# Image scale modulation of a joint image-text attention block: from thin matmul columns to column-tiled rows that VectorE turns into columns

## The chip, the cores and the metric

The kernel runs on one core of a Trainium2 chip. TensorE (PE) does the matmuls and the PE transposes, VectorE (DVE) and ScalarE (ACT) do the elementwise work and empty PSUM, GpSimd (POOL) does small fills, and SyncE (SP) issues nearly all DMAs. The metric is the device time of one execution in microseconds (us), the median of several runs; lower is better. Dates such as "at 14.39" are microseconds from the start of the profiled span.

## What is computed

The sizes are B = 2 batches, 256 image tokens, 32 text tokens, D = 1152 = 9 × 128, all in bfloat16. For the image side (the text side is the same with its own weights):

```
mod  = silu(c) @ wmod_img                 # six vectors of D per batch; three are used
sh, sc, ga = mod[0], mod[1], mod[2]       # shift, scale, gate
h    = layernorm(x_img) * (1 + sc) + sh
q, k, v = split(h @ wqkv_img)
```

Text and image q, k and v are joined, softmax(q k^T / sqrt(D)) v is formed, and each side ends with `out = x + ga * (a @ wo)`. Every weight matrix is read once from HBM; 40.86 MB move in one execution.

## The kernel before, in words

**Weights.** A weight tile is `[128 partitions, 9, 1152]`: "row kt" of a tile below means the 128 rows of the matrix with index kt (288 KB), all 1152 columns. Five slots (`w0` to `w4`) are used in turn. SP issues the loads in program order (lines 103 to 122): two for `x_img`, four for the scale weights `w_sc_i` (rows 0-3, 4-6, 7 and 8), four for the image V weights `w_v_i` (row 0, rows 1-2, rows 3-5, rows 6-8), then one whole tile each for the image shift weights `w_sh_i`, for `w_q_i`, and so on. A load into a slot that was used before waits until its readers are done.

**Modulation columns.** `c` comes in as 18 rows, goes through silu on ACT, and one PE transpose makes it columns: `sT` holds `[128, 9, 2]`, one column per (kt, batch). `sT32` is the same padded to 32 columns with zeros. `sc_cols` (line 214) makes 1 + sc in the form "feature on the partition": for each row kt of `w_sc_i` nine matmuls of a 128×128 block of weights with the two moving columns of `sT`. A first matmul, of a matrix of 1/128 with ones, puts the 1 into PSUM. The result `sc_ps` is `[128, 9, 2]` in PSUM.

The shift goes another way: `mod_rows_of` (line 309) uses `sT32[:, kt, :]` as stationary matrix (32 columns) and lets the weights stream as moving operand. The array is split into four column strips of 32; strip g takes the columns that lie in quarter g of each 128, 288 in all, and writes partitions 32g to 32g+31. A DVE transpose of 32×32 blocks (`mod_cols_of`, line 317) then turns these rows into columns `[128, 9, 32]`, of which the first two are the batches.

**Image tokens.** Four token tiles of 128 are normalised (`xn_i`), batch 0 first. `x_transposes(k0, b)` (line 223) turns three feature blocks of one batch by six PE transposes into a PSUM tile, and returns the function that copies this tile to `xT_i` (ACT, or DVE for k0 = 3). These PSUM tiles alternate between two buffers (`ps_tr`), so the third tile of batch 1 takes the buffer of its first, and its transposes wait for that copy. `x_scale(k0, k1, b)` (line 237) multiplies `xT_i` by 1 + sc on DVE, one instruction per feature block, and writes `hS_i`. The shift is not added there: V is computed without it, and `sh @ w_v` is added later.

**V.** `v_open` (line 247) multiplies `hS_i` by `w_v_i`, 512 output columns a matmul, into PSUM accumulators. `A0` names the four of batch 0, `A1` two of batch 1. The order, lines 281 to 301, is written out by hand:

```
    sc_cols(4, 7)
    out01 = x_transposes(0, 1)
    sc_cols(7, K8); sc_cols(K8, KT)        # K8 = 8, KT = 9
    out31 = x_transposes(3, 1)
    out01(); x_scale(0, 3, 0, sc_ps); sc1_i <- sc_ps
    v_open(A0, 0, 3)
    out61 = x_transposes(6, 1)
    out31(); out61(); the other x_scale
    v_open(A1, 0, 3); v_open(A0 + A1, 3, 7); ...
```

`pin` (line 58) keeps an instruction in program order among the pinned ones; all matmuls and transposes on PE and most of the early DVE and ACT work are pinned, while `mod_cols_of` is not. `warm_up(n)` (line 136) is n matmuls of a constant tile whose result nobody reads; they stand where PE would idle.

**Afterwards** the shift is made from `w_sh_i` and added (`xT_i` becomes the modulated input), V is finished, then come q and k (`qk_img`), the text side, whose shift is formed on DVE while PE works on q and k, then scores, softmax, attention output and output projection. In the text side `txt_cols_shift` and `txt_modulate` (lines 431 to 445) call `mod_cols_of` too and build `hT_t`, which the text q and k matmuls read.

Of the kernel before, what the change touches and what calls it, by code (L numbers as in the profile page):

```python
# [9 lines left out]
ALU = mybir.AluOpType  # L10
# [4 lines left out]
def kernel(  # L15
# [14 lines left out]
    nc = tc.nc  # L30
    bf = mybir.dt.bfloat16
    f32 = mybir.dt.float32
    PSUM = bass.MemoryType.PSUM

    B, NI, D = x_img.shape
    NT = x_txt.shape[1]
    P = 128
    KT = D // P
# [13 lines left out]
    const = ctx.enter_context(tc.tile_pool(name="const", bufs=1))  # L52
    work = ctx.enter_context(tc.tile_pool(name="work", bufs=2))
    small = ctx.enter_context(tc.tile_pool(name="small", bufs=4))
    ps_mm = ctx.enter_context(tc.tile_pool(name="ps_mm", bufs=6, space=PSUM))
    ps_tr = ctx.enter_context(tc.tile_pool(name="ps_tr", bufs=2, space=PSUM))

    pin = tc.keep_in_program_order

    def mm(*a, **k):  # L60
        return pin(nc.tensor.matmul(*a, **k))  # L61

    def tr(*a, **k):
        return pin(nc.tensor.transpose(*a, **k))  # L64
# [11 lines left out]
    def wtile(slot):  # L76
        return wpool.tile([P, KT, D], bf, tag="w%d" % slot, name="t")
# [4 lines left out]
    K8 = KT - 1  # L82
# [17 lines left out]
    w_sc_i = wtile(0)  # L100
# [5 lines left out]
    SCC = (0, 4, 7, K8, KT)  # L106
    for r0, r1 in zip(SCC, SCC[1:]):
        nc.sync.dma_start(w_sc_i[:, r0:r1, :], sc_v[:, r0:r1, :])  # L108
    for r0, r1 in ((0, 1), (1, 3), (3, 6), (6, KT)):
        nc.sync.dma_start(w_v_i[:, r0:r1, :], v_v[:, r0:r1, :])  # L110
    w_sh_i = load_w(2, wmod_img, 0)
    w_q_i = load_w(3, wqkv_img, 0)
# [12 lines left out]
    eps_t = eps_row[:, 0:1]  # L125
    nc.vector.memset(eps_row[:], EPS)
    warm = const.tile([P, 512], bf)
    nc.vector.memset(warm[:], 0.0)  # L128
    unit = const.tile([P, P + B * KT], bf)
    nc.gpsimd.memset(unit[:, 0:P], 1.0 / P)  # L130
    nc.gpsimd.memset(unit[:, P:], 1.0)
    ident = const.tile([P, P], bf)
    make_identity(nc, ident[:])
    wps = ps_mm.tile([P, 512], f32, tag="mm")
# [1 line left out]
    def warm_up(n):  # L136
        for _ in range(n):
            mm(wps[:], lhsT=warm[:, 0:P], rhs=warm[:], start=True, stop=True)

    warm_up(8)  # L140
    sT32 = const.tile([P, KT, 32], bf)
# [15 lines left out]
    sT_ps = ps_tr.tile([P, B * KT], bf, tag="tr")  # L157
    tr(sT_ps[:], s18[:], ident[0:B * KT, 0:B * KT])
    sT = const.tile([P, KT, B], bf)
    warm_up(17)  # L160

    def silu_cols():
        pin(nc.vector.tensor_copy(sT[:], sT_ps[:].rearrange("p (b kt) -> p kt b", b=B)))
# [42 lines left out]
    hS_i = act.tile([P, KT, B * NI], bf, tag="Bt")  # L206
    xT_i = act.tile([P, KT, B * NI], bf)

    sc1_i = const.tile([P, KT, B], f32)
    qkT = act.tile([P, 2 * KT, B, NTOK], bf, tag="Q")  # L210

    sc_ps = ps_mm.tile([P, KT, B], f32, tag="mm")

    def sc_cols(r0, r1):
        if r0 == 0:
            mm(sc_ps[:].rearrange("p kt b -> p (kt b)"), lhsT=unit[:, 0:P], rhs=unit[:, P:],
               start=True, stop=False, skip_group_check=True)
        for kt in range(r0, r1):
            for j in range(KT):
                mm(sc_ps[:, j, :], lhsT=w_sc_i[:, kt, j * P:(j + 1) * P], rhs=sT[:, kt, :],  # L220
                   start=False, stop=(kt == KT - 1), skip_group_check=True)

    def x_transposes(k0, b):
        tr_pool = b == 1 or k0 < 6
        tp = (ps_tr if tr_pool else ps_mm).tile([P, 3, NI], bf, tag="tr" if tr_pool else "mm", name="tp")
        for kt in range(k0, k0 + 3):
            for t in range(TPB):
                i = b * TPB + t
                tr(tp[:, kt - k0, t * P:(t + 1) * P], xn_i[:, i, kt * P:(kt + 1) * P], ident[:])
        dst = xT_i[:, k0:k0 + 3, b * NI:(b + 1) * NI]  # L230

        def copy_out():
            pin(nc.vector.tensor_copy(dst, tp[:]) if k0 == 3 else nc.scalar.copy(dst, tp[:]))

        return copy_out

    def x_scale(k0, k1, b, sc=None):
        sc = sc1_i if sc is None else sc
        for kt in range(k0, k1):
            pin(nc.vector.tensor_scalar(hS_i[:, kt, b * NI:(b + 1) * NI], xT_i[:, kt, b * NI:(b + 1) * NI],  # L240
                                        sc[:, kt, b:b + 1], None, op0=ALU.mult))

    VW = 512
    v_i = act.tile([P, NIT, D], bf, tag="A")
# [2 lines left out]
    def v_open(ids, k0, k1, kt_major=True):  # L247
        for key in ids:
            if key not in accs:
                accs[key] = ps_mm.tile([P, VW], f32, tag="mm", name="vps")  # L250
        loop = [(kt, key) for kt in range(k0, k1) for key in ids] if kt_major else \
            [(kt, key) for key in ids for kt in range(k0, k1)]
        for kt, (i, cc) in loop:
            mm(accs[(i, cc)][:], lhsT=hS_i[:, kt, i * P:(i + 1) * P], rhs=w_v_i[:, kt, cc * VW:(cc + 1) * VW],
               start=(kt == 0), stop=(kt == KT - 1), skip_group_check=True)
            if kt == KT - 1:
                evac(v_i[:, i, cc * VW:(cc + 1) * VW], accs[(i, cc)][:])
# [20 lines left out]
    ln_norm(x_i[:, 2, :], s2[:, 0:1], r2, P, xn_i[:, 2, :])  # L278
    for out in [x_transposes(k0, 0) for k0 in (0, 3, 6)]:
        out()  # L280
    sc_cols(0, 4)
    warm_up(5)
    sc_cols(4, 7)
    out01 = x_transposes(0, 1)
    sc_cols(7, K8)
    sc_cols(K8, KT)
    out31 = x_transposes(3, 1)
    out01()
    x_scale(0, 3, 0, sc_ps)
    pin(nc.vector.tensor_copy(sc1_i[:], sc_ps[:]))  # L290
    v_open(A0, 0, 3)
    out61 = x_transposes(6, 1)
    out31()
    out61()
    for k0 in (0, 3, 6):
        for b in range(B):
            if k0 or b:
                x_scale(k0, k0 + 3, b)
# [1 line left out]
    v_open(A0 + A1, 3, KT - 2)  # L300
    v_open(A0 + A1, KT - 2, KT, kt_major=False)

    NGG = 4
    LW = P // NGG

    def group(w, kt, g):
        return w[:, kt, :].rearrange("p (c g l) -> p g c l", g=NGG, l=LW)[:, g]

    def mod_rows_of(w, lhs):
        gps = ps_tr.tile([P, KT, LW], f32, tag="tr")  # L310
        for kt in range(KT):
            for g in range(NGG):
                mm(gps[LW * g:LW * g + LW], lhsT=lhs[:, kt, :], rhs=group(w, kt, g),
                   start=(kt == 0), stop=(kt == KT - 1), tile_position=(0, LW * g))
        return gps

    def mod_cols_of(gps, name):
        t = const.tile([P, KT, LW], f32, name=name)
        nc.vector.transpose(t[:].rearrange("p c l -> p (c l)"), gps[:].rearrange("p c l -> p (c l)"))
        return t  # L320

    v_open([(2, 1)], 0, KT)
    p_sh = mod_rows_of(w_sh_i, sT32)
    sh_i = mod_cols_of(p_sh, "shc")
    nc.vector.tensor_copy(shT32[:, :, 0:B], sh_i[:, :, 0:B])
    hT_i = xT_i
    for kt in range(KT):
        for b in range(B):
            h = hT_i[:, kt, b * NI:(b + 1) * NI]
            if b == 0 or kt % 3 == 0:  # L330
                nc.vector.tensor_scalar(h, h, sc1_i[:, kt, b:b + 1], sh_i[:, kt, b:b + 1],
                                        op0=ALU.mult, op1=ALU.add)
# [19 lines left out]
    def qk_img(wq, blk, hooks):  # L352
        for j in range(KT):
# [3 lines left out]
            for kt in range(KT):  # L357
# [4 lines left out]
    gsc = tc.dram_tile([2, B, D], bf, name="mod_scratch")  # L362
    sel = const.tile([P, NGG, NTT], bf)
    nc.gpsimd.tensor_scalar(sel[:].rearrange("p g (b t) -> p g b t", b=B),
                            ident[:].rearrange("p (g r) -> p g r", g=NGG)[:, :, 0:B].unsqueeze(3)
                            .to_broadcast([P, NGG, B, NT]), -1.0, None, op0=ALU.mult)
    v_t = act.tile([P, D], bf)
    nc.gpsimd.memset(v_t[NTT:P, :], 0.0)
    svr = act.tile([P, KT, LW], bf)
    rows, cols = {}, {}  # L370

    def shift_v_rows():
        p_sv = mod_rows_of(w_v_i, shT32)
        nc.scalar.copy(svr[:], p_sv[:])
        cols["v"] = mod_cols_of(p_sv, "svc")
# [55 lines left out]
    def txt_cols_shift():  # L431
        cols["sh"] = mod_cols_of(rows["sh"], "shtc")
        nc.vector.tensor_copy(mod_t[:, 0], cols["sh"][:, :, 0:B])
# [26 lines left out]
    def v_txt():  # L460
        for r in range(2):
            ps = ps_mm.tile([P, KT, LW], f32, tag="mm")
            for kt in range(KT):
                for g in range(2):
                    mm(ps[64 * g:64 * g + NTT], lhsT=hT_t[:, kt, :], rhs=group(w_v_t, kt, 2 * r + g),
                       start=(kt == 0), stop=False, tile_position=(0, 64 * g))
            for g in range(2):
                mm(ps[64 * g:64 * g + NTT], lhsT=sel[:, 2 * r + g, :], rhs=svr[:],
                   start=False, stop=True, tile_position=(0, 64 * g))
            for g in range(2):  # L470
                evac(v_t[0:NTT, :].rearrange("p (c g l) -> p g c l", g=NGG, l=LW)[:, 2 * r + g],
                     ps[64 * g:64 * g + NTT])
# [201 lines left out]
```

## Time and profile before

| What | Value |
|---|---|
| Median of 6 runs | 121.54 us (121.17 to 122.17) |
| The profiled execution's own time | 121.27 us |
| Its span | 119.5 us |
| PE busy | 113.9 us (95%), 1105 matmuls |
| DVE, ACT, POOL busy | 74.0, 42.3, 11.6 us |
| Bytes moved, mean rate | 40.86 MB, 342 GB/s |
| PE first matmul of V | at 14.40 |
| PE last matmul chain | ends at 115.48 |

The profile is one execution. Its span of 119.5 us leaves 1.77 us of the execution's own 121.27 us outside, and this execution lies 0.27 us under the median. A busy PE in the table means that matmuls were under way. A single matmul of 512 columns shows 379 ns, but they overlap, and a stream of them starts one every 215 ns; so rates are read from stretches, not from the duration of one. "SPq" is the queue in which SP issues DMAs. A DMA's landing is the issue time plus its time to landing.

### The profile page before, as it was taken

How to read it: one execution, taken by the hardware profiler on the slowest of the kernel's cores; microseconds unless marked ns; L12 is line 12 of the kernel's file. 1: busy time of each engine (PE TensorE's matmuls, PEld its weight loads, DVE VectorE, ACT ScalarE, POOL GpSimd, SP SyncE). 2: the span in 40 equal slices, each digit the busy share in tenths (PEclk: the TensorE clock that was granted, in tenths of full speed). 3: DMA queues.
4: the chain of work that ended last, by engine and by line, in shares of the span. 5: the costliest groups of instructions: out<-in, count | busy, mean ns of one | idle time of the engine just before them, and what ended most of it. 6: DMA issues, size and time to landing. Idle time of an engine off the chain costs nothing.

```text
span 119.5 us, 2609 instructions
## 1 busy us (share of the span) xinstructions
PE 113.9 (95%) x1105; PEld 66.9 (56%) x1105; DVE 74.0 (62%) x155; ACT 42.3 (35%) x86; POOL 11.6 (10%) x34
## 2 busy tenths in 40 slices
PE   5999999999999999999999999999999999999980
PEld 2346744445574444445444457886777766567660
DVE  1568492053867799999999700017785746666670
ACT  4799402031662523323049132335347610000000
POOL 8240000000000000000000000000210806200000
PEclk9999999999999999999999999999999999999999
DMA  3999999999999999999999999999999992420222
GB/s 125 380 378 395 403 404 414 410 412 413 402 404 394 400 411 412 410 413 413 413 405 410 411 414 410 409 410 403 416 408 403 413 383 76 157 99 0 99 67 81
DMA packets 18517, 40.86 MB, mean 342 GB/s; under 512 B 923, under 2 KB 1451, under 8 KB 18507
## 3 DMA queue, kind: packets, MB, share of 16 engines
q1 hardware_dynamic: 17632, 39.56, 85.0%
q0 software_dynamic: 480, 0.89, 2.0%
q10 hardware_dynamic: 395, 0.26, 0.7%
q8 instruction: 8, 0.13, 0.4%
q14 instruction: 2, 0.02, 0.0%
HBM read 39.38 MB, written 1.34 MB: 341 GB/s over the span
## 4 chain that ended last, share of the span: by engine, by line
PE 84%; DMA 8%; SPq 2%; DVE 2%; issue 1%; DVEq 0%
PE ps L61 52%; PE vps L61 14%; DMA t<-in_wmod_img_dram 8%; PE aps L61 6%; PE gps L61 6%; PE sps L61 4%; SPq L108 1%; DVE hS_i L240 1%; PE pT_ps L64 1%; SPq L104 1%; DVE tmp L615 1%; DVE o L616 0%; PE sc_ps L61 0%; PE tpt L64 0%; PE tp L64 0%
## 5 line engine op out<-in xcount | busy, mean ns | idle before, releaser
L61 PE MATMUL ps<-xT_i,t 128*128 128x512 bf16 x162 | 35.8, 379 | 0.0
L61 PEld LDWEIGHTS <-t 128*128 128x128 bf16 x405 | 22.7, 98 | 20.1 <-DMA t<-in_wmod_img_dram 0.9
L398 DVE SCALAR_TENSOR_TENSOR acc_sh<-t,sTf,acc_sh 128x1152 f32<-128x1152 bf16 x16 | 21.3, 1401 | 0.0
L61 PE MATMUL ps<-t,aT 128*128 128x384 bf16 (+3 forms) x153 | 20.2, 308 | 0.0
L61 PE MATMUL vps<-t,hS_i 128*128 128x512 bf16 (+1 forms) x108 | 18.2, 326 | 0.4 <-DVE hS_i L240 0.3
L61 PEld LDWEIGHTS <-aT 128*128 128x128 bf16 (+1 forms) x153 | 13.0, 101 | 7.1 <-issue 0.5
L61 PEld LDWEIGHTS <-hS_i 128*128 128x128 bf16 x108 | 8.9, 98 | 9.0 <-issue 0.8
L615 DVE TENSOR_TENSOR tmp<-ps,gb 128x384 bf16<-128x384 f32 (+2 forms) x13 | 6.8, 526 | 6.3 <-PE ps L61 5.0
L348 ACT ACTIVATE qkT<-ps 128x512 bf16<-128x512 f32 (+2 forms) x11 | 6.2, 563 | 12.3 <-PE ps L61 12.3
L483 POOL DMA_DIRECT2D mod_scratch<-g_sb x4 | 2.5, 634 | 78.4 <-ACT g_sb L173 78.4
L61 PE MATMUL wps<-warm 128*128 128x512 bf16 x30 | 8.3, 433 | 1.2 <-DVE warm L128 1.2
L350 ACT CAST qkT<-ps 128x512 bf16<-128x512 f32 (+2 forms) x11 | 5.9, 554 | 8.6 <-PE ps L61 8.6
L171 DVE CAST v_i<-vps 128x512 bf16<-128x512 f32 x5 | 3.5, 691 | 7.6 <-PE vps L61 7.6
L171 DVE CAST v_t<-ps 64x288 bf16<-64x288 f32 x2 | 0.9, 459 | 11.7 <-ACT v_t L173 11.7
L61 PE MATMUL aps<-pT,v_i 128*128 128x288 bf16 x36 | 6.7, 287 | 0.0
L587 DVE TENSOR_SCALAR aT<-aps,svc 128x288 bf16<-128x288 f32 x9 | 4.7, 518 | 2.4 <-PE aps L61 2.3
L61 PEld LDWEIGHTS <-warm 128*128 128x128 bf16 x30 | 3.0, 109 | 5.0 <-issue 1.6
L61 PE MATMUL sps<-qkT 128*128 128x288 bf16 (+1 forms) x54 | 5.5, 287 | 0.0
L589 ACT ACTIVATE aT<-aps,svc 128x288 bf16<-128x288 f32 x9 | 4.5, 501 | 2.5 <-PE aps L61 2.5
L61 PE MATMUL aps<-pT,v_t 128*128 128x288 bf16 x18 | 5.1, 286 | 0.0
L61 PE MATMUL gps<-t,sT 128*32 128x288 bf16 x144 | 5.1, 287 | 0.0
L61 PE MATMUL ps<-hT_t,t 128*128 128x64 bf16 x162 | 5.0, 193 | 0.0
(106 smaller groups left out, 108.7 us busy)
## 6 DMA issues: line engine op xcount, KB each, us to landing
t<-in_wqkv_txt_dram SPq DMA_DIRECT2D x3, 2592.0 KB, 15.7
t<-in_wmod_img_dram SPq DMA_DIRECT2D x2, 2592.0 KB, 16.4
t<-in_wqkv_img_dram SPq DMA_DIRECT2D x2, 2592.0 KB, 19.8
t<-in_wmod_txt_dram SPq DMA_DIRECT2D x2, 2592.0 KB, 14.8
t<-in_wmod_txt_dram SPq DMA_DIRECT2D x3, 864.0 KB, 16.1
t<-in_wo_img_dram SPq DMA_DIRECT2D x1, 2592.0 KB
t<-in_wo_txt_dram SPq DMA_DIRECT2D x1, 2592.0 KB, 19.8
t<-in_wqkv_img_dram SPq DMA_DIRECT2D x2, 864.0 KB, 13.8
```

Of the source, the lines that this page charges most:

```text
L61: return pin(nc.tensor.matmul(*a, **k))
L64: return pin(nc.tensor.transpose(*a, **k))
L104: nc.sync.dma_start(x_i[:, b * TPB:(b + 1) * TPB, :], x_img[b].rearrange("(p t) d -> p t d", t=TPB))
L108: nc.sync.dma_start(w_sc_i[:, r0:r1, :], sc_v[:, r0:r1, :])
L171: nc.vector.tensor_copy(out_ap, in_ap)
L348: nc.scalar.mul(out_ap, in_ap, SCALE)
L350: nc.scalar.copy(out_ap, in_ap)
L398: pin(eng.scalar_tensor_tensor(acc[:, b, :], w[:, kt, :], sTf[:, kt, b:b + 1], acc[:, b, :], op0=ALU.mult, op1=ALU.add))
L483: nc.gpsimd.dma_start(gsc[si, b, :].rearrange("(g j) -> g j", g=NGG), g_sb[b:P:32, :])
L587: nc.vector.tensor_scalar(dst, aps[:], bias, None, op0=ALU.add)
L589: nc.scalar.activation(dst, aps[:], ACT.Identity, bias=bias)
L615: nc.vector.tensor_mul(tmp[:, 0:n], ps[:, 0:n], gb[:, b, c0:c0 + n])
```

## The change

- `sc_cols` becomes `sc_rows`: the scale is formed as the shift is. `sT32` is stationary, the weights stream, four column strips with 288 moving columns each: 4 matmuls per row kt where there were 9. The 1 is put in by 4 matmuls of `unit` (now 32 columns of 1/128) with `warm`, which now holds ones.
- `mod_cols_of` moves up, is pinned on DVE, and turns the rows into `sc1_i` `[128, 9, 32]`. The copy of `sc_ps` to `sc1_i` goes, and the first `x_scale` reads `sc1_i` from SBUF too. Two text results share buffers with the image columns that are done by then.
- The third group of batch-1 transposes, `x_transposes(6, 1)`, stands ahead of the first V matmuls and no longer behind them.
- `w_v_i` is loaded in six pieces (rows 0, 1, 2, 3-4, 5-6, 7-8) in place of four.
- `warm_up` goes from 17 to 14, and from 5 to 3 and 1. The fills of `unit` go from POOL to DVE.

```diff
-    for r0, r1 in ((0, 1), (1, 3), (3, 6), (6, KT)):
+    for r0, r1 in ((0, 1), (1, 2), (2, 3), (3, 5), (5, 7), (7, KT)):
         nc.sync.dma_start(w_v_i[:, r0:r1, :], v_v[:, r0:r1, :])
...
-    nc.vector.memset(warm[:], 0.0)
-    unit = const.tile([P, P + B * KT], bf)
-    nc.gpsimd.memset(unit[:, 0:P], 1.0 / P)
-    nc.gpsimd.memset(unit[:, P:], 1.0)
+    nc.vector.memset(warm[:], 1.0)
+    NGG = 4
+    LW = P // NGG
+    unit = const.tile([P, LW], bf)
+    nc.vector.memset(unit[:], 1.0 / P)
...
-    warm_up(17)
+    warm_up(14)
...
-    sc1_i = const.tile([P, KT, B], f32)
-    sc_ps = ps_mm.tile([P, KT, B], f32, tag="mm")
-
-    def sc_cols(r0, r1):
+    def group(w, kt, g):
+        return w[:, kt, :].rearrange("p (c g l) -> p g c l", g=NGG, l=LW)[:, g]
+
+    def mod_cols_of(gps, name):
+        t = const.tile([P, KT, LW], f32, name=name, tag={"shtc": "scc", "sctc": "shc"}.get(name, name))
+        pin(nc.vector.transpose(t[:].rearrange("p c l -> p (c l)"), gps[:].rearrange("p c l -> p (c l)")))
+        return t
+
+    sc_ps = ps_mm.tile([P, KT, LW], f32, tag="mm")
+
+    def sc_rows(r0, r1):
         if r0 == 0:
-            mm(sc_ps[:].rearrange("p kt b -> p (kt b)"), lhsT=unit[:, 0:P], rhs=unit[:, P:],
-               start=True, stop=False, skip_group_check=True)
+            for g in range(NGG):
+                mm(sc_ps[LW * g:LW * g + LW].rearrange("p c l -> p (c l)"), lhsT=unit[:], rhs=warm[:, 0:KT * LW],
+                   start=True, stop=False, tile_position=(0, LW * g))
         for kt in range(r0, r1):
-            for j in range(KT):
-                mm(sc_ps[:, j, :], lhsT=w_sc_i[:, kt, j * P:(j + 1) * P], rhs=sT[:, kt, :],
-                   start=False, stop=(kt == KT - 1), skip_group_check=True)
+            for g in range(NGG):
+                mm(sc_ps[LW * g:LW * g + LW], lhsT=sT32[:, kt, :], rhs=group(w_sc_i, kt, g),
+                   start=False, stop=(kt == KT - 1), tile_position=(0, LW * g))
...
-    sc_cols(0, 4)
-    warm_up(5)
-    sc_cols(4, 7)
+    sc_rows(0, 4)
+    warm_up(3)
+    sc_rows(4, 7)
+    warm_up(1)
     out01 = x_transposes(0, 1)
-    sc_cols(7, K8)
-    sc_cols(K8, KT)
+    sc_rows(7, K8)
+    sc_rows(K8, KT)
     out31 = x_transposes(3, 1)
+    sc1_i = mod_cols_of(sc_ps, "scc")
     out01()
-    x_scale(0, 3, 0, sc_ps)
-    pin(nc.vector.tensor_copy(sc1_i[:], sc_ps[:]))
+    x_scale(0, 3, 0)
+    out61 = x_transposes(6, 1)
     v_open(A0, 0, 3)
-    out61 = x_transposes(6, 1)
     out31()
     out61()
```

More of the change, by code (lines that the diff above doesn't have):

```diff
@@ L235, in x_transposes, with x_scale @@
         return copy_out
-    def x_scale(k0, k1, b, sc=None):
-        sc = sc1_i if sc is None else sc
+    def x_scale(k0, k1, b):
         for kt in range(k0, k1):
             pin(nc.vector.tensor_scalar(hS_i[:, kt, b * NI:(b + 1) * NI], xT_i[:, kt, b * NI:(b + 1) * NI],
-                                        sc[:, kt, b:b + 1], None, op0=ALU.mult))
+                                        sc1_i[:, kt, b:b + 1], None, op0=ALU.mult))
     VW = 512
@@ L301 @@
     v_open(A0 + A1, KT - 2, KT, kt_major=False)
[L303 to L307, printed above, removed]
     def mod_rows_of(w, lhs):
@@ L315, in mod_rows_of @@
         return gps
[L317 to L320, printed above, removed]
     v_open([(2, 1)], 0, KT)
```

## Prediction, made before the result was known

> **What bounds the kernel now.** I read the page first (busy shares, then the chain that ended last), then the chain in order of time, and then the timeline of the stretch in which the chain is not PE.
>
> ```profile
> PE 113.9 (95%) x1105; PEld 66.9 (56%) x1105; DVE 74.0 (62%) x155; ACT 42.3 (35%) x86; POOL 11.6 (10%) x34
> ...
> PE 84%; DMA 8%; SPq 2%; DVE 2%; issue 1%; DVEq 0%
> ```
>
> PE is busy for 95% of the span and holds 84% of the chain. What is not PE lies almost wholly at the start. The chain in order of time (start, length, what):
>
> ```profile
> 3.47 10.04 DMA t<-in_wmod_img_dram
> ...
> 13.56 0.39 PE sc_ps L61 x9
> ...
> 14.05 0.69 DVE hS_i L240 x3
> ...
> 15.69 1.89 PE vps L61 x8
> 17.58 0.34 PE tp L64 x6
> 17.91 11.01 PE vps L61 x51
> 28.92 1.22 PE gps L61 x36
> ```
>
> Row 8 of the scale weights lands at 13.51 (issued at 3.47, 10.04 us). PE finishes the scale, DVE scales three blocks, V begins. From 15.69 the chain is PE without a break to 115.48. So the change is worth what it does to the moment from which PE runs without a hole, plus the PE work that it puts before or behind that moment.
>
> The timeline of that stretch (start, length, engine, line, operation; in brackets the idle time before):
>
> ```profile
> 13.28 0.80 ACT L233 COPY xT_i<-tp 128x768 bf16<-128x768 bf16 x1 [0.70 <-PE tp L64]
> ...
> 13.80 0.50 PE L64 MATMUL tp<-ident,xn_i 128*128 128x128 bf16 x6
> 14.05 0.69 DVE L240 TENSOR_SCALAR hS_i<-xT_i,sc_ps 128x256 bf16<-128x256 bf16 x3 [1.71 <-PE sc_ps L61]
> ...
> 14.40 1.04 PE L61 MATMUL vps<-t,hS_i 128*128 128x512 bf16 x4
> ...
> 15.69 1.89 PE L61 MATMUL vps<-t,hS_i 128*128 128x512 bf16 x8 [0.26 <-DVE hS_i L240]
> ...
> 17.41 0.50 PE L64 MATMUL tp<-ident,xn_i 128*128 128x128 bf16 x6
> ```
>
> Eight V matmuls take 17.41 − 15.69 = 1.72 us, 0.215 each. Four from 14.40 would be through at 15.26, but the next starts at 15.69: a hole of 0.43 us. The page names DVE, but `hS_i` for kt 0 to 2 was done at 14.74, so it was the DMA of rows 1-2 of `w_v_i`. Six transposes take 0.34 us (17.75 − 17.41), so those of 13.80 end at 14.14, and PE waits 0.26 for DVE. PE's holes here are 0.26 + 0.43 = 0.69 us; closing both is all that there is to win.
>
> **The change part by part.** The operations that it adds exist in before, where the shift is made:
>
> ```profile
> 28.85 0.98 PEld L61 LDWEIGHTS <-sT 128*32 128x32 bf16 x36 [0.42 <-issue]
> 28.85 1.29 PE L61 MATMUL gps<-t,sT 128*32 128x288 bf16 x36
> ...
> 30.07 1.47 PE L61 MATMUL vps<-t,hS_i 128*128 128x512 bf16 x6
> 30.19 0.48 DVE L319 STREAM_TRANSPOSE shc<-gps 128x288 f32<-128x288 f32 x1 [0.54 <-PE gps L61]
> ...
> 30.77 0.17 DVE L325 CAST shT<-shc 128x18 bf16<-128x18 f32 x1
> ```
>
> 36 strip matmuls of 0.29 us span 1.29, so one starts every 1.00/35 = 0.029 us. From the last start (29.85) to the next full-width matmul (30.07) is 0.22; before the first there is 0.10 (the last V slot ends at 28.75).
>
> *PE up to the scale.* Rows 4-6 land at 12.02: 12 strip matmuls start from 12.06 to 12.38, one warm-up from 12.60, the transposes of (0, batch 1) from 12.82 (12.74 before), their copy on ACT from 13.36 to 14.16. Row 7 follows at 13.25 and fits. Row 8 lands at 13.51 as before, since nothing ahead of it in the queue changes; its four matmuls start from 13.56 to 13.65 and end at 13.94, against 13.95 for the nine thin ones. No gain and no loss on the path. The transposes of (3, 1) follow at 13.65 + 0.22 = 13.87, to 14.21; those of (6, 1) need ACT's copy (14.16, so about 14.21) and end at 14.55.
>
> *DVE.* Before, the first scaling started at 14.05 and V at 14.40, 0.35 later. Now the block transpose stands ahead: it starts 0.05 (as at 30.14 to 30.19) to 0.10 (13.95 to 14.05) after PE, takes 0.48, and the instruction that reads it starts 0.04 (`shtc` at 67.10, its reader at 67.62) to 0.10 (30.67 to 30.77) after it. 13.94 + 0.05 to 0.10 + 0.48 + 0.04 to 0.10 + 0.35 = 14.86 to 14.97; I take 14.92. V starts **0.52 later**. The dropped copy (0.17) stood behind the scalings and was hidden.
>
> *V and its rows.* Row 0 landed at 14.26 (3.96 + 10.3). Rows 1-2 were in at 15.69 as one piece; now kt 1 is wanted at 14.92 + 0.86 = 15.78 and kt 2 at 16.64. Even the old piece would be in time: the hole of 0.43 goes because V starts late, and the split adds nothing (bounds: nothing, and below nothing the 0.43 if V could start at 14.40, which DVE excludes). Twelve matmuls run to 14.92 + 12 × 0.215 = 17.50. The transposes (0.34) no longer follow, as they lie in PE's wait for DVE, which without them would be idle; without that cover they cost their 0.34 again. So PE is at 17.50 where it was at 17.75: **0.25 us earlier** (0.20 to 0.31 by the bounds). Check: −0.43 − 0.34 + 0.52 = −0.25.
>
> *What is late next.* Batch 1's first three scalings are wanted at 17.50. DVE does three scalings from 14.57, the copy of (3, 1) (0.55), then these three at 0.20: done about 16.4. The copy of (6, 1), before at 17.95, starts near 14.8. Nothing of DVE or ACT is late.
>
> *Rest of the span.* Each later weight must be there 0.25 earlier. Issue plus time to landing gives: `w_sh_i` 26.6 for 28.85, `w_q_i` 33.2 for 35.34, `w_sc_t` 53.1 for 55.34, `w_ga_t` 85.3 for 87.28. The least slack is 2.0 us. So the 0.25 is kept.
>
> *Text side.* The transposes on DVE are now pinned. In before `sctc` ran at 63.95, ahead of its place; now it stands behind `shtc`. The chain from 67.10 is 0.48 + 0.48 + 0.15 + 0.76 + 0.76 with the copy of 0.17 and gaps, done near 70.1; PE wants `hT_t` at 70.88 (both move by 0.25). Cost nothing, but a slack of 2.3 becomes 0.8.
>
> *SP.* Two more issues of 0.45 to 0.47 us. The queue also shows a limit: `w_sh_i` is issued at 9.88, just after rows 0-3 of the scale landed (1.64 + 8.2), and `w_q_i` at 12.03, just after rows 4-6 (2.11 + 9.9), each eight loads behind the one that it waits for. With two loads more, rows 5-6 are issued at about 9.9, rows 7-8 at 12.0 and `w_sh_i` near 12.9, 3 to 6 us later. Bounds: nothing, if landing is set by the bytes ahead; 2.4 us, if a piece takes as long from its issue as rows 6-8 did (14.3): rows 7-8 at 26.3, wanted at 18.79 + 24 × 0.215 = 23.95. I take nothing: nine rows (2.65 MB, 6.5 us at 405 GB/s) still lie ahead at 12.0, and a load of 576 KB into an empty queue took 3.7 us.
>
> *Fills and warm-ups.* `unit` on DVE is in the shade of the DMAs (DVE idles from 1.17 to 4.07). Fewer warm-ups leave PE idle from 4.51 + 14 × 0.215 = 7.52 to 8.61, and from about 11.2 to 12.06. Cost nothing, if the clock holds. Before it held over idle times up to 0.4 us; the eight first matmuls ran at 0.427 each (weight loads at 2.48, 2.91, 3.34) and all later ones at 0.215.
>
> [...]
>
> **The sum.** Span 119.5 − 0.25 = 119.25, the execution's own 121.27 − 0.25 = 121.02. It lies 0.27 under the median, so the median becomes 121.54 − 0.25 = **121.3 us**.
>
> **The rivals.**
> 1. *No gain: V stands in PE's queue behind transposes that wait for ACT.* The (6, 1) group waits for ACT's copy of (0, 1). The gain is gone if V starts at 15.17, that is if the copy ends at 14.78 rather than 14.16. For it: three engines hand over in a row. Against: 0.37 us of slack (14.55 to 14.92), and ACT is idle from 12.58. Time 121.5 to 121.7. Chance 0.16.
> 2. *Faster: V starts as early as before and rows come singly.* Then both holes and the transposes go: 17.75 − (14.40 + 2.58) = 0.77, so 120.8. It needs a DVE transpose of next to nothing, against the row of 0.48. Chance 0.08.
> 3. *Slower: the last pieces of the V weights come late*, as they are issued 4 to 6 us later. The place is kt 7 at 23.95; each microsecond of landing after that is one lost, and past 24.2 the gain is eaten. At the upper bound 121.3 + 2.4 = 123.7. Against: the DMA share is full throughout, so landing is set by bytes. Chance 0.07.
> 4. *Slower clock.* A fall to 0.427 a matmul in the new idle times, lasting as long as the first eight: 8 × 0.212 = 1.7, so 123.0. Chance 0.05.
>
> **How the numbers follow.** The forecast has 0.64. The range of 120.7 to 122.0 holds it with the spread of runs about their median before (−0.37 to +0.63), rivals 1 and 2, and leaves out 3 and 4. About 0.5% (0.6 us) is what a measurement of this kernel can tell from no change. Faster by more: rival 2 and a little, 0.10; slower by more: rivals 3 and 4, 0.12; within: 0.78.
>
> **What would show it.** In the changed profile: the scale ends near 13.94; a block transpose of 0.48 on DVE; V's first matmul near 14.92; no hole between its 4th and 5th matmul; the 13th at 17.50; the shift's strips at 28.6; transposes of (6, 1) before V. V starting after 15.17 means rival 1, a hole at kt 5 to 8 rival 3, V matmuls 0.427 apart rival 4. A stall of PE at 70.6 would say that the pinned text chain was undercosted.

## The result, and the profile after

The changed kernel takes 121.03 us in the median of 24 runs (120.33 to 121.39), the kernel before 121.51 us (48 runs). The ratio is 0.9955, with a 95% interval of 0.9942 to 0.9968: 0.55 us faster (0.39 to 0.70; 0.48 by the medians), where 0.25 had been forecast. A ratio leaves out executions more than 1.5% over the fastest of their kernel. The profiled execution took 121.04 us, its span is 119.2.

The same lines of the page as before: busy time by engine, and the chain by engine.

```profile
PE 113.1 (95%) x1059; PEld 65.4 (55%) x1059; DVE 74.8 (63%) x156; ACT 42.2 (35%) x86; POOL 11.4 (10%) x32
...
PE 86%; DMA 8%; DVE 2%; SPq 1%; issue 0%; DVEq 0%
```

The chain of the changed kernel in order of time (start, length, what):

```profile
2.10 10.10 DMA t<-in_wmod_img_dram
...
13.45 0.24 PE sc_ps L61 x4
...
13.71 0.33 PE sc_ps L61 x4
14.04 0.02 issue
14.06 0.49 DVE scc L217
...
14.65 0.30 DVE hS_i L248
14.95 0.05 issue
15.00 13.77 PE vps L61 x63
28.77 1.22 PE gps L61 x36
```

The shape is the forecast one: rows of the scale, one block transpose on DVE, one scaling, then all 63 V matmuls in one stretch without a hole and without transposes in it. V starts at 15.00 and the shift's strips on PE at 28.70, against 28.85 before.

But row 8 of the scale weights was multiplied at 13.71 here and at 13.56 in the profile of before. Over all profiles of this study in which that DMA sets the date, it lies between 13.03 and 13.92. Two profiles are therefore compared from this date on. From the first matmul of row 8 to the strips, before needs 28.85 − 13.56 = 15.29 us and the changed kernel 28.70 − 13.71 = 14.99: **0.30 us less in this stretch**, where 0.25 was worked out. The runs show 0.55. So the stretch behaves as forecast, and by these two profiles some 0.25 us came from elsewhere.

### The profile page after: what moved, and what is told of

Its sections match the earlier page's. It is cut to its first block, busy times and chain, and to the rows that moved or that the text cites. A ratio compares the mean times of both kernels' runs of the same rounds, so it can differ in the third digit from the quotient of the medians.

```text
span 119.2 us, 2516 instructions
## 1 busy us (share of the span) xinstructions
PE 113.1 (95%) x1059; PEld 65.4 (55%) x1059; DVE 74.8 (63%) x156; ACT 42.2 (35%) x86; POOL 11.4 (10%) x32
## 4 chain that ended last, share of the span: by engine, by line
PE 86%; DMA 8%; DVE 2%; SPq 1%; issue 0%; DVEq 0%
PE ps L61 52%; PE vps L61 15%; DMA t<-in_wmod_img_dram 8%; PE aps L61 6%; PE gps L61 6%; PE sps L61 4%; PE sc_ps L61 1%; PE pT_ps L64 1%; SPq L104 1%; DVE tmp L613 1%; DVE o L614 0%; DVE scc L217 0%; SPq L108 0%; PE tpt L64 0%; PE tp L64 0%
## 5 line engine op out<-in xcount | busy, mean ns | idle before, releaser
L61 PEld LDWEIGHTS <-t 128*128 128x128 bf16 x324 | 20.4, 98 | 19.2 <-issue 0.7
L61 PEld LDWEIGHTS <-sT 128*32 128x32 bf16 x180 | 4.5, 96 | 3.2 <-issue 2.7
L174 ACT CAST v_i<-vps 128x512 bf16<-128x512 f32 x4 | 2.3, 581 | 10.0 <-PE vps L61 10.0
## 6 DMA issues: line engine op xcount, KB each, us to landing
t<-in_wqkv_txt_dram SPq DMA_DIRECT2D x3, 2592.0 KB, 16.1
t<-in_wmod_img_dram SPq DMA_DIRECT2D x2, 2592.0 KB, 13.6
```

What stands on the lines that cost most here:

```text
L174: nc.scalar.copy(out_ap, in_ap)
```

## The experiments

Two theories stood at first: that of the prediction (the rows cost 0.52, the hole and the moved transposes give 0.43 and 0.34, nothing else counts), and its rivals that the missing 0.25 comes from the rows themselves or from the split. Later the warm-ups came in. Each kernel was timed against the kernel before, on the same chip.

### The parts, put into the kernel before

**Transposes of (6, 1) ahead of V, alone.**

```diff
-    v_open(A0, 0, 3)
     out61 = x_transposes(6, 1)
+    v_open(A0, 0, 3)
```

> The kernel before with one part alone, the transposes of (6, 1) ahead of V. Theory of the prediction: they end near 14.5, V's first four end before rows 1-2 land at 15.7 as ever, so the 0.34 of the transposes is gained: 121.15 to 121.2. Rival 'split' and rival 'rows' both say less than the theory only if PE waits for the copy on ACT; then 121.4 to 121.5.

121.06 us, ratio 0.9980 (0.9962 to 0.9998). PE's timeline (start, length, operation):

```profile
13.84 0.86 PE L64 MATMUL tp<-ident,xn_i 128*128 128x128 bf16 x12
14.54 1.03 PE L61 MATMUL vps<-t,hS_i 128*128 128x512 bf16 x3
15.73 12.89 PE L61 MATMUL vps<-t,hS_i 128*128 128x512 bf16 x58 [0.17 <-DVE hS_i L240]
28.55 1.29 PE L61 MATMUL gps<-t,sT 128*32 128x288 bf16 x36
```

All twelve transposes stand before V, and V starts 0.14 later than before (four matmuls from 14.54, one record is missing). The hole ahead of 15.73 is still there, shorter by what V starts later; so PE's wait for DVE and a part of the hole now cover the transposes. From row 8 (13.60) to the strips: 14.95 us, 0.34 less than before, to the hundredth what the transposes take.

**The split of the V weights, alone.**

```diff
-    for r0, r1 in ((0, 1), (1, 3), (3, 6), (6, KT)):
+    for r0, r1 in ((0, 1), (1, 2), (2, 3), (3, 5), (5, 7), (7, KT)):
```

> The kernel before with the six pieces alone. Theory of the prediction: V starts 0.84 after the first matmul of row 8, kt 1 is wanted 0.86 later and row 1 is then in, so the hole of 0.43 closes: 0.43 under before, ratio 0.9965, and eight rows of four V matmuls without a break. Rival 'queue' (two more loads, later issues cost something): less than 0.2 gained.

120.52 us, ratio 0.9959 (0.9942 to 0.9977).

```profile
14.12 2.76 PE L61 MATMUL vps<-t,hS_i 128*128 128x512 bf16 x11
16.72 0.50 PE L64 MATMUL tp<-ident,xn_i 128*128 128x128 bf16 x6
```

Twelve V matmuls run from 14.12 to 16.72 (one record is missing) with no hole. From row 8 (13.28) to the strips (28.16): 14.88, 0.41 less than before. The rival 'queue' falls. In a kernel where V starts early, the split alone is worth nearly the whole change.

**Both, with the thin columns kept.** The two diffs together.

> The kernel before (thin scale columns) with two of the parts alone: the six pieces, and the transposes of (6, 1) ahead of V. Theory of the prediction: the rows and their transpose on DVE cost 0.52 and give nothing, so without them V starts near 14.5, finds its rows landed one by one, and the 13th V matmul starts near 17.06: 0.69 under before, 120.8, and 0.2 to 0.45 under the changed kernel. Rival 'rows': the dense rows themselves bring time, so this is slower than the changed kernel, 121.2 or more.

120.64 us, ratio 0.9940 (0.9919 to 0.9961); all its executions lie between 120.12 and 120.71. Its chain in order of time:

```profile
13.16 0.38 PE sc_ps L61 x9
13.54 0.73 PE tp L64 x12
14.26 0.22 PE vps L61
...
27.86 1.22 PE gps L61 x36
```

V follows the transposes at once; DVE is no longer on this part of the chain. From row 8 to the strips (27.79): 14.63 us, 0.66 less than before and 0.36 less than the changed kernel. It was run a second time, beside the last experiments:

> The thin kernel with six pieces and early transposes (old warm-ups) once more, so that the other three stand beside it on one chip. Theory of the prediction for the rows: 0.69 under before, ratio 0.9943.

120.57 us, ratio 0.9924 (0.9904 to 0.9945). Both times its ratio is below that of the changed kernel; the intervals touch (0.9919 to 0.9961 and 0.9942 to 0.9968), and the two were not timed on one chip, so I call it the best kernel here by its traces, and by the runs the likely one.

### The parts, taken out of the changed kernel

**The old four pieces.** The diff of the split, reversed.

> The changed kernel with the old four pieces of the V weights (rows 0, 1-2, 3-5, 6-8). Theory of the prediction: V starts near 15.0, rows 1-2 are in by 15.9, so the split is worth nothing: 121.0 to 121.1, as the changed kernel (121.03). Rival 'split': the 0.23 us that the sum lacks (0.48 measured, 0.25 forecast) come from rows that land singly: 121.25 to 121.3, and a hole in PE between the 4th and the 5th V matmul. Rival 'rows': no matter for it, 121.0 to 121.1.

121.02 us, ratio 0.9974 (0.9957 to 0.9990), which touches the interval of the changed kernel: by the runs unclear. The weight loads of PE (of `hS_i`, the stationary side) show a small hole:

```profile
14.31 0.76 PEld L61 LDWEIGHTS <-hS_i 128*128 128x128 bf16 x5 [0.38 <-DVE hS_i L248]
15.33 1.17 PEld L61 LDWEIGHTS <-hS_i 128*128 128x128 bf16 x6 [0.26 <-issue]
```

The fifth V matmul was due at 14.32 + 4 × 0.215 = 15.18 and starts at 15.33. Its block of `hS_i` was loaded early (five loads from 14.31), so by elimination it waited for rows 1-2 of `w_v_i`; the profile names no releaser there. The prediction had found them in time by 0.09; they are late by 0.15. So the split is worth up to 0.15 in the changed kernel. From row 8 (13.03) to the strips (28.16): 15.13, 0.14 more than the changed kernel.

**The transposes behind V again.**

```diff
-    out61 = x_transposes(6, 1)
     v_open(A0, 0, 3)
+    out61 = x_transposes(6, 1)
```

> The changed kernel with the transposes of (6, 1) behind the first twelve V matmuls, as before. Theory of the prediction: they lose their cover and cost 0.34: 0.34 over the changed kernel, about level with before (ratio 0.999 to 1.001). Rival: they are hidden either way, level with the changed kernel.

120.91 us, ratio 0.9979 (0.9963 to 0.9996), against 0.9954 (0.9937 to 0.9971) for the changed kernel on the same chip (below): 0.30 us lost, 0.34 expected, with intervals that overlap. The traces settle it. Here PE comes to row 8 when it is already in, so another event has to date the profile: with six pieces SP issues `w_q_i` just after row 8 has landed. In the changed kernel row 8 is issued at 3.62 and takes 10.1 us, and `w_q_i` is issued at 13.68, 0.03 before the first matmul of row 8.

```profile
13.68 3.68 SPq L89 DMA_DIRECT2D t<-in_wqkv_img_dram  x1
```

From there to the strips the changed kernel needs 28.70 − 13.68 = 15.02, this one 28.12 − 12.77 = 15.35: 0.33 more. That the transposes are hidden either way falls. By the runs it is not level with before, though: 0.25 stay as a gain that the sum does not know.

**Both taken out: rows, fills and warm-ups alone.**

> The changed kernel with the old four pieces and with the transposes of (6, 1) behind the first twelve V matmuls as before: what is left of the change is the scale as rows, the fills and the warm-ups. Theory of the prediction: -0.43 + 0.52 = +0.09, 121.6, that is no gain. Rival 'rows': a gain of 0.15 or more from the rows or from the fewer warm-ups, 121.35 or less.

121.22 us, ratio 0.9989 (0.9968 to 1.0010). Inconclusive between +0.09 and −0.15 by the runs. By its trace from row 8 (13.92) to the strips (29.24): 15.32, 0.03 more than before. The rows bring nothing to this stretch. The 0.25 from elsewhere should show here too; the interval allows it, but does not show it.

### The warm-ups

**The changed kernel again**, as a measure for its neighbours.

> The changed kernel once more, beside the three that follow on one chip. By its profile, counted from the first matmul of row 8 of the scale weights, it is 0.30 us ahead of before (28.70 - 13.71 against 28.85 - 13.56); by the first timing 0.55 (0.39 to 0.70). Theory of the prediction: 0.25 to 0.35 under before, ratio 0.997 to 0.998. Rival 'more than this stretch' (something outside it brings another 0.25): 0.55, ratio 0.9955.

120.56 us, ratio 0.9954 (0.9937 to 0.9971). From row 8 (13.50) to the strips (28.49) 14.99 again. So the 0.55 are real, and by the profiles 0.25 of them lie outside the stretch.

**The old warm-ups in the changed kernel.**

```diff
-    warm_up(14)
+    warm_up(17)
...
-    warm_up(3)
+    warm_up(5)
...
-    warm_up(1)
```

> The changed kernel with the old warm-ups (17, then 5, none before the transposes of (0, 1)). Theory of the prediction: they lie in waits for DMA, level with the changed kernel within 0.1. Rival 'fills': the fewer warm-ups bring the 0.2 that the sum lacks, so this is 0.2 to 0.3 over the changed kernel, with the first transposes or the rows of the scale starting later.

120.76 us, ratio 0.9981 (0.9963 to 0.9998). That is 0.23 us under before, close to the forecast figure, and 0.0027 or 0.33 us over the changed kernel (0.20 by the medians; the two intervals overlap). Its chain shows why:

```profile
11.92 0.65 PE wps L61 x3
12.57 0.48 PE sc_ps L61 x12
13.05 0.46 PE tp L64 x6
13.51 0.02 issue
13.53 0.81 ACT xT_i L242
14.34 0.04 issue
14.38 0.49 PE tp L64 x6
14.88 1.65 PE vps L61 x7
```

No DMA is in it. The warm-ups are late, so the scale rows 4-6 behind them, then the transposes of (0, 1), then their copy on ACT, then the transposes of (6, 1), and V last. This is rival 1 of the prediction, in the form of a queue that fills from its front. It can be priced in this one execution: `w_q_i` is issued at 13.25, so row 8 was in by then, and the strips start at 28.54, that is 15.29 later, 0.27 more than the 15.02 of both profiles of the changed kernel.

```profile
13.25 3.66 SPq L89 DMA_DIRECT2D t<-in_wqkv_img_dram  x1
```

Why are they late? The weight loads of PE in another execution (that of the kernel with rows alone) show by their distance how fast the matmuls start:

```profile
6.40 0.15 PEld L61 LDWEIGHTS <-warm 128*128 128x128 bf16 x1 [0.28 <-issue]
6.83 0.15 PEld L61 LDWEIGHTS <-warm 128*128 128x128 bf16 x1 [0.27 <-issue]
7.25 1.61 PEld L61 LDWEIGHTS <-warm 128*128 128x128 bf16 x8 [0.27 <-issue]
```

Up to 7.25 a warm-up takes 0.43, then eight loads lie in 1.61. So in this execution the full rate came near 7.3; in the profile of before it came at 4.5, in that with the old warm-ups at 6.4, in others between 4.5 and 7.0. (In the six profiles in which the granted clock was read it is 1.00 from the start to 12 us, so this date is read from the distances alone. Where the granted clock itself reads 0.50, further down, weight loads again lie 0.42 apart, at 15.30 and 15.72. That the slow start is a half clock too is my inference from this likeness and was not shown; "clock" in the expectations below means this rate where they speak of the start.) The date changes from one execution to the next. The profile on which the prediction rests is one with the earliest date, and it was 0.24 under the median of all runs of before (121.27 against 121.51). There 17 warm-ups end before the first transposes can start (they end at 8.35, the transposes start at 8.61, PE idle for 0.25); with the full rate at 6.4 the transposes start at 9.49, behind them without a wait. That the same happens in executions of before is inferred, since it has one profile. The nearest sight of it is the second profile of the thin kernel, whose PE work up to row 8 is that of before: its full rate came near 6.1, and its chain runs through the warm-ups, where that of its first profile (5.2) began with row 8's load.

```profile
7.99 1.29 PE wps L61 x6
9.29 1.00 PE tp L64 x18
10.29 0.90 PE sc_ps L61 x37
```

**Six more warm-ups than in the changed kernel**, to make the suspected cost larger. The new theory is called 'queue' (it is not the 'queue' of the loads above): where the full rate comes late, the warm-ups hold up all that stands behind them in PE's queue.

```diff
-    warm_up(14)
+    warm_up(20)
```

> The changed kernel with 20 warm-ups in place of 14, that is 1.29 us more of PE work ahead of the first transposes at 0.215 each. Theory 'queue': the 0.3 of idle time before the first transposes and the 0.7 before rows 4 to 6 of the scale are used up, the copy of (0, 1) on ACT and with it the transposes of (6, 1) and V come late: 0.3 to 0.6 over the changed kernel, ratio to before 0.998 to 1.0005. Theory of the prediction (hidden): level with the changed kernel, 0.9955.

121.20 us, ratio 0.9988 (0.9966 to 1.0011): about 0.4 over the changed kernel by the ratios, as 'queue' says, though the two were not timed on one chip and the intervals touch. Its chain goes through them:

```profile
7.87 1.51 PE wps L61 x7
9.38 1.00 PE tp L64 x18
10.38 0.73 PE sc_ps L61 x20
```

But this profile is the fastest of the twelve executions (120.53), with the full rate from 4.9, and in it nothing is lost: from the issue of `w_q_i` (13.16) to the strips (28.18) are the 15.02 of the changed kernel. The 0.4 rest on the runs alone.

**Fewer warm-ups in the kernel before**, and **in the thin kernel with both parts**.

```diff
-    warm_up(17)
+    warm_up(14)
...
-    warm_up(5)
+    warm_up(3)
```

> The kernel before with fewer warm-ups alone (14 for 17, 3 for 5). New theory 'queue': where TensorE's clock becomes full late, the warm-ups run past the moment at which the first transposes could start, everything behind them in PE's queue is late, and where the weights of the scale land early V starts late; so fewer warm-ups give 0.15 to 0.3, ratio 0.9975 to 0.999. Theory of the prediction: they lie in waits, nothing, ratio 0.9993 to 1.0007.

> The kernel before with six pieces, transposes of (6, 1) ahead of V, and 14 and 3 warm-ups: the change without its rows. Theory 'queue': 0.15 to 0.3 under the same kernel with the old warm-ups, that is 0.85 to 1.0 under before, ratio 0.992 to 0.993, and 0.3 to 0.5 under the changed kernel (0.9955). Theory of the prediction for the warm-ups: ratio 0.9943, level with the same kernel with the old warm-ups (-0.69).

Neither theory foresaw what came. The first has a median of 122.00 us and a spread of 120.60 to 123.11, the second 120.96 and 119.76 to 121.99; before lies at 121.35 beside them. Medians and spreads are used here, not ratios. Each execution lists its mean granted clock. In the first, four of twelve executions have 1.000 and take 120.60 to 121.46; eight have 0.968 to 0.986 and take 121.76 to 123.11. In the second, three have 0.997 or more (119.76 to 120.41) and three 0.981 (121.52 to 121.99). The executions with the full clock bear 'queue' out, few as they are and picked by their clock: their medians are 120.94, 0.41 under before, and 120.36, 0.21 under the thin kernel with the old warm-ups. The profile of the second caught one of the latter. Its busy time by stretch (each line: the stretch, its length, five engines' busy time with their instructions in brackets, then clock, DMA share and GB/s):

```profile
core 0: us, PE busy (x) PEld busy (x) DVE busy (x) ACT busy (x) POOL busy (x), PEclk, DMA share, GB/s
...
12.00:12.50 0.50, 0.50 (x24) 0.50 (x24) 0.28 (x1) 0.50 (x1) 0.00 (x0) 1.00 1.01 378
12.50:13.00 0.50, 0.50 (x15) 0.50 (x12) 0.00 (x0) 0.01 (x1) 0.00 (x0) 0.71 1.06 401
13.00:13.50 0.50, 0.50 (x16) 0.50 (x15) 0.00 (x0) 0.15 (x1) 0.00 (x0) 0.50 1.00 387
...
15.50:16.00 0.50, 0.28 (x2) 0.15 (x1) 0.50 (x4) 0.41 (x1) 0.00 (x0) 0.50 0.94 369
16.00:17.00 1.00, 1.00 (x5) 0.39 (x4) 1.00 (x7) 0.00 (x0) 0.00 (x0) 0.94 1.01 387
```

The weight loads of V in the slow stretch:

```profile
15.30 0.15 PEld L61 LDWEIGHTS <-hS_i 128*128 128x128 bf16 x1 [0.28 <-issue]
15.72 0.15 PEld L61 LDWEIGHTS <-hS_i 128*128 128x128 bf16 x1 [0.28 <-issue]
```

The clock falls to half near 12.7 and is full again near 16.1, worked out from 0.71 and 0.94, so V begins (14.87) in the slow stretch. This is rival 4's mechanism, and it fell on a kernel with thin columns and few warm-ups, not on the changed one: in its 36 executions of both timings the mean clock is never below 0.994.

## Why the prediction was right in direction and half the size

| Kernel | row 8 to strips, us | against before | worked out |
|---|---|---|---|
| before | 15.29 | | |
| changed (two profiles) | 14.99, 14.99 | −0.30 | −0.25 |
| transposes early alone | 14.95 | −0.34 | −0.34 |
| changed, old four pieces | 15.13 | −0.16 | −0.25 |
| split alone | 14.88 | −0.41 | −0.43 |
| both, thin columns | 14.63 | −0.66 | −0.69 |
| rows, fills and warm-ups alone | 15.32 | +0.03 | +0.09 |
| before with fewer warm-ups | 15.31 | +0.02 | 0 |

- *The stretch around V* was right term by term, within 0.07. The block transpose took 0.48; V came 15.00 − 13.71 = 1.29 after row 8, 14.92 − 13.56 = 1.36 was worked out. The rows are a loss on this path, as said: with them the stretch is 0.36 longer than without (14.99 against 14.63).
- *The split adds nothing*: right only within a margin that was too narrow. 0.09 in hand were forecast; with the old pieces 0.15 are missing in one profile (old pieces) and none in the other (rows alone).
- *Rest of the span kept*: right. PE's last matmul chain ends at 115.33 against 115.48, so the 0.15 between the two profiles goes through unchanged.
- *SP, rival 3*: `w_sh_i` was issued at 12.98 (forecast 12.9) and took 13.6 to land where it had taken 16.7: 26.6, the same date as before. By then 9.78 MB had moved, before 9.80, so in these two profiles the landing went with the bytes moved and not with the issue; rival 3 fell.
- *Text side*: the pinned chain ended at 69.07 + 0.76 = 69.83, PE wanted it at 70.73. The slack is 0.90, forecast 0.8. No stall:

```profile
66.95 0.48 DVE L217 STREAM_TRANSPOSE shtc<-gps 128x288 f32<-128x288 f32 x1 [1.24 <-PE gps L61]
...
67.56 0.47 DVE L217 STREAM_TRANSPOSE sctc<-gps 128x288 f32<-128x288 f32 x1
...
69.07 0.76 DVE L442 TENSOR_TENSOR hT_t<-hT_t,mod_t 128x576 bf16<-128x576 bf16 x1
```

- *"Fills and warm-ups … Cost nothing"*: **this is the term that was mis-sized.** It was put at nothing; taking the warm-ups back costs 0.33 us by the ratios (0.9981 against 0.9954), 0.20 by the medians, and 0.27 in the one profile. They were taken for idle filling because the one profile of before had its full rate from 4.5. In other executions they are work at the head of PE's queue. −0.30 from the stretch and −0.20 to −0.33 from the warm-ups cover the −0.55 that was measured; the second figure is the less certain one.
- *"If the clock holds"*: it held (0.994 or more in all 36 executions), but that was luck. The prediction judged by PE's idle times, and by these the thin kernels with fewer warm-ups are no worse: the longest wait is 0.46 us in the profile with the fall and 0.73 in the changed kernel's. Yet in one of them the clock fell in eight of twelve executions. Rival 4's condition, an idle time of PE, therefore does not tell these profiles apart (see below). Nor did the forecast idle time of 1.09 ahead of the first transposes come: it was 0.30, as the 14 warm-ups started at 5.14 and not at 4.51.

What stays open: why the fewer warm-ups are safe in the changed kernel and not in that before. One candidate is the strips, which move 288 columns where the thin matmuls move two, but the changed kernel also has one more warm-up ahead of the (0, 1) transposes and warm-ups of ones rather than zeros; these were not tried apart. If it is the strips, the rows buy the shorter warm-up, and that is their worth: on the path they cost.

## What to carry to other kernels

One profile is one draw: where the start of a kernel depends on when the matmuls reach their full rate (here 4.5 to 7.3) or a load lands (row 8 was multiplied at 13.03 to 13.92), compare profiles from a common event, and do not call work hidden because one draw hid it. A big gain may sit in a small part: here splitting one load and moving six transposes, two edits of one line each, gave more by the traces, and likely by the runs (0.9940 and 0.9924), than the whole rewrite (0.9955). Filler work had two sides here: the old warm-ups cost the changed kernel 0.20 to 0.33 us, and with fewer of them the old kernel had a mean clock of 0.968 to 0.986 in eight of twelve executions (0.994 or more in all 23 with the old ones, timed beside it). Judge it by the spread and the mean clock of many runs, not by the median alone; the one profile of that kernel had a clock of 1.00.

## What the runs showed of the hardware

- The clock fell while PE was busy: from 12.5 to 13.0 its busy time is 0.50 of 0.50 us and the mean granted clock 0.71. In the profile with the fall PE's busy share was 0.92 from 10 to 11 us and 0.54 from 11 to 12, with one wait of 0.46 us. In the changed kernel's profile it was 0.99 and 0.51 with a wait of 0.73 us, and the granted clock stayed at 1.00 up to 20 us; so the busy shares of these stretches do not tell the two apart, and what does stays open. From 2 us to the fall the longest wait of PE is 0.46 us, and the fall began, near 12.7, in a stretch of matmuls of two columns (27 from 11.90, 18 from 13.11) and transposes (6 from 12.59, 12 from 13.63). It lasted to 16.1, that is 3.4 us.
- Filling the warm-up tile with ones took DVE 0.485 us where zeros, written as 128x256 uint32, had taken 0.272. With the fill of `unit` behind it, PE's first matmul started at 1.49 rather than 1.23.

```profile
0.94 0.48 DVE L128 MEMSET warm<- 128x512 bf16 x1
```

- In the changed kernel SP issued rows 5-6 at 10.06, just after the load eight places ahead had landed (rows 0-3 of the scale, 1.62 + 8.4 = 10.02); `w_sh_i`, at 12.98, and `w_q_i`, at 13.68, followed rows 7 and 8 of the scale likewise (2.94 + 10.0 = 12.94 and 3.62 + 10.1 = 13.72, the landing times being rounded). 3.1 us of later issue (12.98 against 9.88) did not move the landing of `w_sh_i` (26.6) while the DMA share was 0.97 to 1.07 (in stretches from 4.5 to 20 us).
